# Attention and feed-forward on one core: attention first and alone, x kept in DRAM, feed-forward after it

## The chip, the cores and the metric

The kernel runs on one core of a Trainium2 chip. The core has five engines with a queue of their own each: PE (matrix multiply, with its weight loads shown as PEld), DVE (vector), ACT (scalar functions), POOL, and SP, which here only issues DMAs. They are kept in step by semaphores. Matmuls write to PSUM, eight banks of 512 fp32 values for each of 128 partitions; everything else lies in SBUF. The metric is the device time of one execution in microseconds (us); lower is better.

## The reference

```python
def phi(x):                                    # q, k: 8 x 8 heads x 576 x 64; w_phi: 64 x 128
    proj = np.einsum('bhsd,df->bhsf', x, w_phi)
    proj = proj - np.max(np.abs(proj), axis=-1, keepdims=True)
    return np.concatenate([np.exp(proj), np.exp(-proj)], axis=-1)
q_p, k_p = (phi(q), phi(k))
kv = np.einsum('bhsf,bhsd->bhfd', k_p, v)
z = np.sum(k_p, axis=2)
num = np.einsum('bhsf,bhfd->bhsd', q_p, kv)
den = np.einsum('bhsf,bhf->bhs', q_p, z)[..., None] + 1e-06
x = num / den                                  # as 4608 tokens x 512
h = x @ w_in                                   # 512 x 2048
g = h * np.tanh(np.log1p(np.exp(h)))           # Mish
out = g @ w_out                                # 2048 x 512
```

The weights of the feed-forward come as float64.

## The kernel before

**Attention** is cut into 36 units of 512 (token, head pair) rows of k and 36 of q; two units of q make one chunk c of 256 tokens. A unit of k is loaded and projected into PSUM (`pp_k`, `project`, L158), DVE takes the row maximum of the absolute value (`m`, L173) and subtracts it (`e`, L174), ACT makes both exponentials (L215, L216), and PE sums exp times v into `kvps` (`k_sum`, L183; v has a column of ones, which gives z). A finished pair's `kvps` is copied to `kv` (L232). A unit of q is projected the same way (`pp_q`), turned by PE (`dt`, `q_turn`, L250), put through both exponentials (L252), multiplied with `kv` into `num` (`q_num`, L183), divided (`r`, L267 and L268; `x`, L269), and turned once more into `xt` (`q_out`, L277). ACT and DVE split `xt` into a rounded part `xTh` and a rest `xTl`, which stay in SBUF.

**The feed-forward** works on 18 chunks times 16 tiles f of 128 hidden columns, 288 tiles in all. `ff_in` (L299) makes a tile of `h` with 12 matmuls of 256 columns: four pieces of x, times three products of high and low parts. For each pair of tiles `mish` (L302) has ACT compute Mish into `u` and round it to `gh`, and DVE take the rest `gl` (L312). `ff_out` (L329), LAG tiles later, adds g times w_out into two banks `o`: 6 matmuls of 512 columns a tile.

**The weights** are 32 pieces of 128 x 512 float64 numbers. `split_weight` (L109) makes a high and a low fp32r part of one piece: ACT takes the absolute value of the upper words (L118), DVE clamps, shifts, masks and joins (L120 to L126), ACT rounds (L130), DVE subtracts and adds (L134, L135). For the first 16 pieces (`summed`) the last two are done by PE instead (`sum_weight`, L139: matmuls with the identity into a bank, copied out by ACT).

**Order.** Only PE's order is written out by hand: every piece of work gets a time in tiles (`at`), the events are sorted, and PE runs them in that order. The other engines' orders come out of a scheduler at build time. FIRST_STEPS, WLOADS and WTIMES place the first attention steps and the weights; from the fourth unit on, one unit of attention goes with 8 tiles of the feed-forward, so the two are interleaved to the end. The first two chunks go through the feed-forward in halves of 8 tiles (NHALVED), with partial sums in `part`, as the later weights come late.

**PSUM** has three pools: four banks `ps_att`, two `ps_h` (one pair of h tiles in each bank), two `ps_o`.

Of the kernel before, what the change touches and what calls it, by code (L numbers as in the profile page):

```python
# [52 lines left out]
def attention_then_mish(ctx, tc, qT, kT, va, w_phi, w_in, w_out, out):  # L53
# [15 lines left out]
    nc.sync.dma_start(w_phi2, w_phi)


    pieces = [("in", i, 0) for i in range(NCC)]
    for j in range(1, 4):
        pieces += [("out", 4 * (j - 1) + i, 0) for i in range(4)] + [("in", i, j) for i in range(NCC)]
    pieces += [("out", 12 + i, 0) for i in range(4)]
    weight = {}
    starting = True

    spare = [f"w{kind}_{i}_{j}" for kind, i, j in pieces[-NSPARE:]]

    def slot_tile(slot, dtype, name):
        return const.tile([P, 2, 512], dtype, tag=slot, name=name)

    def spare_tile(n, dtype, name):
        return slot_tile(spare[n], dtype, name)

    ident_r = spare_tile(0, F32R, "ident_r")[:, :, :P]
    for k in range(2):
        nc.scalar.activation(ident_r[:, k, :], ident, AF.Copy, scale=1.0 - 2 * k)
    raws = {}  # L90

    def raw_tile(name):

        n = len(raws)
        raws[n] = None
        if n >= NRAWSPARE:
            return work.tile([P, 512], F32, tag="raw", name=name, bufs=NRAW)
        if n % 2 == 0:
            raws[n] = spare_tile(1 + n // 2, F32, name)
        return (raws[n] if n % 2 == 0 else raws[n - 1])[:, n % 2, :]  # L100

    def load_weight(kind, i, j):
        nm = f"{kind}_{i}_{j}"
        src = w_in[i * P:(i + 1) * P, j * 512:(j + 1) * 512] if kind == "in" else w_out[i * P:(i + 1) * P, :]
        words = slot_tile(f"w{nm}", U32, f"words_{nm}").rearrange("p a b -> p (a b)")
        nc.sync.dma_start(words, src.bitcast(U32))
        weight[kind, i, j] = words.rearrange("p (a b) -> p a b", b=2)

    def split_weight(kind, i, j, summed):  # L109


        nm = f"{kind}_{i}_{j}"
        words = weight[kind, i, j]
        low, high = words[:, :, 0], words[:, :, 1]
        w = moe.tile([P, 512], U32, tag="u", name=f"w_{nm}", bufs=3)
        t = work.tile([P, 512], F32, tag="half", name=f"t_{nm}", bufs=NHALF)
        wf = w.bitcast(F32)
        nc.scalar.activation(wf, high.bitcast(F32), AF.Abs)  # L118

        nc.vector.tensor_scalar(wf, wf, LARGE, SMALL, op0=ALU.min, op1=ALU.max)  # L120
        nc.vector.tensor_scalar(w, w, 3, 0x3FFFFFF8, op0=ALU.logical_shift_left, op1=ALU.bitwise_and)
        nc.vector.scalar_tensor_tensor(w, high, 0xC0000000, w, op0=ALU.bitwise_and, op1=ALU.bitwise_or)

        nc.vector.tensor_scalar(t.bitcast(U32), w, 0xFF800000, None, op0=ALU.bitwise_and)
        rest = work.tile([P, 512], F32R, tag="part", name=f"rest_{nm}", bufs=2 * NHALVED) if summed else t
        nc.vector.scalar_tensor_tensor(rest, low, 2.0 ** -52, t, op0=ALU.mult, op1=ALU.mult)  # L126
        parts = slot_tile(f"w{nm}", F32R, f"w{nm}")
        hi, lo = parts[:, 0, :], parts[:, 1, :]
        weight[kind, i, j] = (hi, lo)
        nc.scalar.copy(hi, wf)  # L130
        if summed:
            to_sum[kind, i, j] = (wf, rest)
        else:
            nc.vector.tensor_sub(wf, wf, hi.bitcast(F32))  # L134
            nc.vector.tensor_tensor(lo, wf, rest, op=ALU.add)  # L135

    to_sum = {}

    def sum_weight(kind, i, j):  # L139
# [3 lines left out]
        nc.tensor.matmul(ps, ident, wf, start=True, stop=False)
# [14 lines left out]
    def project(raw, name, nh):  # L158


        ps = []
        for j in range(2):
            pool, tag = (ps_h, "h") if starting and not nh or j < nh else (ps_att, "att")
            ps.append(pool.tile([P, 4, F], F32, tag=tag, name=f"pp{j}_{name}"))
        for n in range(4):
            for j in range(2):
                rows = slice(j * D, (j + 1) * D)
                nc.tensor.matmul(ps[j][:, n], raw[rows, n * P:(n + 1) * P], w_phi2[rows], start=True, stop=True)  # L168
# [10 lines left out]
    def halves(ps, lhsT, rhs, start, stop):  # L179

        for h in range(2):
            rows = slice(h * D, (h + 1) * D)
            nc.tensor.matmul(ps[rows], lhsT[:, rows], rhs[h], start=start, stop=stop, skip_group_check=True)  # L183
# [245 lines left out]
```

## Time and profile before

| | us |
|---|---|
| median of 3 runs | 1193.73 |
| lowest and highest run | 1188.72, 1194.0 |
| span of the profiled execution | 1190.0 |
| PE busy, PEld busy | 1142.8, 1022.0 |
| ACT busy, DVE busy | 621.4, 480.7 |

Of the profiled execution itself the span is what the profile gives, from its first instruction to its last; it lies among the runs. The profile lists busy time of each engine, the same for any stretch of the span, groups of instructions by source line (`L299 PE MATMUL h<-xTh,win`: line, engine, operation, what is written and read), waits (who waited, and what released him), and the chain that ended last, followed back from the last instruction. In the timeline a row is: start, duration, engine, line, operation, tiles, shapes, count, and in brackets the idle time before it with its releaser. "x16" counts instructions as the chip runs them: an fp32 matmul counts two. Neighbouring operations of an engine overlap, so the distance from start to start is often shorter than the duration.

### The profile page before, as it was taken

What the parts mean: (1) busy time and instruction counts of PE and PEld (TensorE: products, weight loads), DVE (VectorE), ACT (ScalarE), POOL (GpSimd) and SP (SyncE); (2) the same over time, 40 slices, a digit from 0 to 9 for tenths busy, and PEclk for the clock granted to TensorE, in tenths of its full rate; (3) what the DMA queues carried; (4) which work ended last, traced back from release to release, by engine and by line L of the source; (5) the groups of instructions that cost most, each with busy time, mean ns of one, the idle gap of its engine ahead of it and who ended that gap; (6) DMA issues with size and microseconds to landing.
All of it is one profiled execution on the core that took longest, in us unless ns stands there. A gap on an engine that the chain in (4) does not pass through costs nothing.

```text
span 1190.0 us, 26544 instructions
## 1 busy us (share of the span) xinstructions
PE 1142.8 (96%) x11696; PEld 1022.0 (86%) x11696; DVE 480.7 (40%) x1057; ACT 621.4 (52%) x1019; POOL 0.7 (0%) x6
## 2 busy tenths in 40 slices
PE   6888887999999999999999999999999999999998
PEld 5666777999898989898989899989989898898997
DVE  5876987333333333333333333333333332222311
ACT  4567675454555555555555555554545454545422
POOL 0000000000000000000000000000000000000000
PEclk9999987999999999999999999999999999999999
DMA  9901200111111010111111111011111100000000
GB/s 346 375 13 30 74 14 19 48 48 31 48 30 48 27 42 19 41 31 48 30 38 30 48 30 48 19 45 34 34 44 30 48 19 28 1 19 19 1 19 18
DMA packets 25027, 57.51 MB, mean 48 GB/s; under 512 B 2768, under 2 KB 2896, under 8 KB 24912
## 3 DMA queue, kind: packets, MB, share of 16 engines
q1 hardware_dynamic: 24912, 55.81, 14.2%
q8 instruction: 92, 1.51, 0.5%
q14 instruction: 23, 0.19, 0.1%
HBM read 46.37 MB, written 9.44 MB: 47 GB/s over the span
## 4 chain that ended last, share of the span: by engine, by line
PE 83%; ACT 9%; DVE 6%; issue 1%; DMA 1%; SPq 0%; ACTq 0%
PE h L299 32%; PE o L329 29%; PE kvps L183 6%; PE num L183 5%; PE pp_q L168 3%; PE pp_k L168 3%; PE dt L250 2%; ACT L252 2%; ACT e_q L252 1%; PE xt L277 1%; ACT e_k L215 1%; ACT gh L311 1%; ACT u L307 1%; ACT e_k L216 1%; ACT L307 1%
## 5 line engine op out<-in xcount | busy, mean ns | idle before, releaser
L299 PE MATMUL h<-xTh,win 128*128 128x256 f32 x2304 | 465.1, 286 | 8.5 <-DVE e_q L174 5.3
L299 PEld LDWEIGHTS h<-xTh,win 128*128 128x128 f32 x2304 | 377.0, 191 | 22.6 <-issue 5.9
L329 PE MATMUL o<-wout,gh 128*128 128x512 f32 x1152 | 371.8, 404 | 5.5 <-ACT osb L342 4.0
L312 DVE TENSOR_TENSOR gl<-u,gh 128x256 fp32r<-128x256 f32 x288 | 116.7, 424 | 573.0 <-ACT gh L311 564.7
L299 PE MATMUL h<-xTl,win 128*128 128x256 f32 x1152 | 325.9, 283 | 0.0
L329 PEld LDWEIGHTS o<-wout,gh 128*128 128x128 f32 x1152 | 198.7, 190 | 39.1 <-ACT osb L342 9.3
L329 PE MATMUL o<-wout,gl 128*128 128x512 f32 x576 | 228.3, 396 | 0.0
L299 PEld LDWEIGHTS h<-xTl,win 128*128 128x128 f32 x1152 | 219.5, 191 | 8.3
L307 ACT ACTIVATE u<-h 128x512 f32<-128x512 f32 x144 | 86.2, 599 | 171.2 <-PE h L299 165.8
L280 ACT CAST xTh<-xt 128x512 fp32r<-128x512 f32 x36 | 21.2, 589 | 292.3 <-PE xt L277 283.8
L329 PEld LDWEIGHTS o<-wout,gl 128*128 128x128 f32 x576 | 108.9, 189 | 27.4
L311 ACT CAST gh<-u 128x256 fp32r<-128x256 f32 x288 | 110.5, 408 | 19.3 <-PE o L329 6.4
L307 ACT ACT_TABLE_LOAD x73 | 93.7, 1283 | 8.3 <-DVE wout L135 7.0
L183 PEld LDWEIGHTS kvps<-v,e_k 128*64 128x64 f32 x2560 | 82.5, 144 | 13.4 <-issue 11.6
L183 PE MATMUL kvps<-v,e_k 128*64 128x65 f32 x2560 | 87.6, 230 | 0.9 <-ACT e_k L216 0.9
L252 ACT ACTIVATE e_q<-dt 128x512 f32<-128x512 f32 x144 | 77.9, 597 | 16.7 <-PE dt L250 16.4
L252 ACT ACT_TABLE_LOAD x64 | 82.1, 1283 | 1.0
L183 PE MATMUL num<-kv,e_q 128*64 128x65 f32 x2304 | 74.1, 222 | 0.0
L183 PEld LDWEIGHTS num<-kv,e_q 128*64 128x64 f32 x2304 | 70.6, 138 | 2.7 <-issue 2.0
L168 PE MATMUL pp_k<-w_phi,kraw 64*128 64x128 f32 x576 | 49.2, 295 | 20.6 <-issue 9.4
L168 PEld LDWEIGHTS pp_k<-w_phi,kraw 64*128 64x128 f32 x576 | 43.9, 202 | 23.7 <-issue 19.4
L173 DVE TENSOR_REDUCE m_q<-pp_q 128x4 f32<-128x512 f32 x72 | 46.4, 685 | 8.2 <-PE pp_q L168 8.2
(66 smaller groups left out, 756.8 us busy)
## 6 DMA issues: line engine op xcount, KB each, us to landing
v<-va SPq DMA_DIRECT2D x32, 325.0 KB, 3.1
kraw<-kT SPq DMA_DIRECT2D x36, 256.0 KB, 2.7
out<-osb SPq DMA_DIRECT2D x36, 256.0 KB, 2.0
qraw<-qT SPq DMA_DIRECT2D x35, 256.0 KB, 3.0
words_in<-w_in SPq DMA_DIRECT2D x16, 512.0 KB, 8.7
words_out<-w_out SPq DMA_DIRECT2D x16, 512.0 KB, 9.1
kraw<-qT SPq DMA_DIRECT2D x1, 256.0 KB, 8.5
w_phi<-w_phi SPq DMA_DIRECT2D x1, 64.0 KB, 1.7
```

The lines of the kernel that those rows point to most:

```text
L168: nc.tensor.matmul(ps[j][:, n], raw[rows, n * P:(n + 1) * P], w_phi2[rows], start=True, stop=True)
L173: nc.vector.tensor_reduce(m, ps[j], axis=AX.X, op=ALU.max, apply_absolute_value=True)
L183: nc.tensor.matmul(ps[rows], lhsT[:, rows], rhs[h], start=start, stop=stop, skip_group_check=True)
L215: table(nc.scalar.activation(e[:, 1, :], e[:, 0, :], AF.Exp))
L250: nc.tensor.transpose(ps[:, n * P:(n + 1) * P], e[:, 0, n * P:(n + 1) * P], ident)
L252: table(nc.scalar.activation(e[:, s, :], ps, AF.Exp, scale=2.0 * s - 1.0))
L280: nc.scalar.copy(hi, ps)
L299: nc.tensor.matmul(ps, w[:, wcol], x[:, cc % 2, :], start=(n == 0), stop=(n == 11))
L307: table(nc.scalar.activation(u, hv, AF.Mish))
L311: nc.scalar.copy(gh, u[:, f * CH:(f + 1) * CH])
L312: nc.vector.tensor_sub(gl, u[:, f * CH:(f + 1) * CH], gh.bitcast(F32))
L329: nc.tensor.matmul(ps, g[:, cols], w, start=(i == first and k == 0), stop=(i == end and k == 2))
```

## The change

Attention is now run by itself, in 36 steps of 7.3 us (STEP) in PE's hand-written order, with k three units (LEAD) ahead of q. x is turned, copied to SBUF by ACT and stored in a DRAM tile per chunk; the feed-forward loads it back 12 tiles ahead and splits it 6 tiles ahead. The feed-forward follows as one sequence of 288 tiles. Sixteen weight pieces (w_in of j = 0 and 1, w_out of f = 0 to 7) are loaded and split during attention, the other sixteen after it, into a pool that takes over attention's SBUF. All 32 are summed on DVE; `sum_weight` is gone. Four chunks (NSPLIT) go in halves.

A projection now takes a tile of two banks for both heads (`ps_a`, two tiles), and max, subtraction and exponentials run over 1024 elements at once. The `h` of four tiles f share such a two-bank tile. The other four banks (`ps_b`) hold kvps, dt, num and xt, and later o. `gh` and `gl` are made for a pair of tiles at once. The copy to `kv` goes to ACT.

```diff
-NRAW, NE, NV, NKV = 4, 6, 2, 10
-NHALF, NX, NXT, NG = 2, 2, 4, 4
...
-LAG, TAIL, TAILLAG = 4, 10, 2
+LEAD = 3
+STEP = 7.3
+TILE = 2.82
+LAG = 5
+NSPLIT = 4
...
-    ps_att = ctx.enter_context(tc.tile_pool(name="ps_att", bufs=4, space=PSUM))
-    ps_h = ctx.enter_context(tc.tile_pool(name="ps_h", bufs=2, space=PSUM))
-    ps_o = ctx.enter_context(tc.tile_pool(name="ps_o", bufs=2, space=PSUM))
+    ps_a = ctx.enter_context(tc.tile_pool(name="ps_a", bufs=2, space=PSUM))
+    ps_b = ctx.enter_context(tc.tile_pool(name="ps_b", bufs=4, space=PSUM))
...
+    x_spill = [tc.dram_tile([P, NCC, CH], F32, name=f"x_spill_{c}") for c in range(NCH)]
...
-    def sum_weight(kind, i, j):
...
-    def project(raw, name, nh):
+    def project(raw, name):
+
+        ps = ps_a.tile([P, 2, 4, F], F32, tag="pp", name=f"pp_{name}")
         for n in range(4):
             for j in range(2):
                 rows = slice(j * D, (j + 1) * D)
-                nc.tensor.matmul(ps[j][:, n], raw[rows, n * P:(n + 1) * P], w_phi2[rows], start=True, stop=True)
...
+                nc.tensor.matmul(ps[:, j, n], raw[rows, n * P:(n + 1) * P], w_phi2[rows], start=True, stop=True)
+        e = att.tile([P, 2, 2, 512], F32, tag="e", name=f"e_{name}", bufs=5)
+        m = att.tile([P, 2, 4], F32, tag="m", name=f"m_{name}", bufs=4)
+        nc.vector.tensor_reduce(m, ps, axis=AX.X, op=ALU.max, apply_absolute_value=True)
+        nc.vector.tensor_tensor(e[:, :, 0, :].rearrange("p j (n f) -> p j n f", f=F), ps,
+                                m.unsqueeze(3).broadcast_to([P, 2, 4, F]), op=ALU.subtract)
...
-                    nc.vector.tensor_copy(kv[p // NHP, p % NHP], kv_ps.pop(p))
+                    nc.scalar.copy(kv[p // NHP, p % NHP], kv_ps.pop(p))
...
-        nc.scalar.copy(hi, ps)
-        nc.vector.tensor_sub(lo, ps, hi.bitcast(F32))
-        xT[c, g] = (hi, lo)
+        xs = att.tile([P, 2, CH], F32, tag="xs", name=f"xs_{n}", bufs=3)
+        nc.scalar.copy(xs, ps)
+        nc.sync.dma_start(x_spill[c][:, 2 * g:2 * g + 2, :], xs)
...
+    def x_load(c):
+        x32 = ffn.tile([P, NCC, CH], F32, tag="x32", name=f"x32_{c}", bufs=2)
+        nc.sync.dma_start(x32, x_spill[c])
+        xT[c] = x32
+
+    def x_split(c, again):
+        x32 = xT[c]
+        hi = ffn.tile([P, NCC, CH], F32R, tag="xTh", name=f"xTh_{c}_{again}", bufs=2)
+        lo = ffn.tile([P, NCC, CH], F32R, tag="xTl", name=f"xTl_{c}_{again}", bufs=2)
+        nc.scalar.copy(hi, x32)
+        nc.vector.tensor_sub(lo, x32, hi.bitcast(F32))
+        xT[c] = (hi, lo)
...
+    for u in range(NU):
+        t = (u - LEAD) * STEP
+        at(t - 2 * STEP, k_load, u)
+        at(t - STEP, v_load, u)
+        at(t, k_proj, u)
+        at(t + 0.1, k_exp, u)
+        at(t + STEP + 2.0, k_sum, u)
+        t = u * STEP
+        at(t - 2 * STEP, q_load, u)
+        at(t + 1.0, q_proj, u)
+        at(t + STEP + 6.3, q_turn, u, 0)
+        at(t + STEP + 6.8, q_turn, u, 1)
+        at(t + 2 * STEP + 4.0, q_num, u)
+        at(t + 3 * STEP + 6.0, q_out, u)
+    early = [("in", i, j) for j in range(2) for i in range(NCC)]
+    early = [p for n in range(8) for p in (early[n], ("out", n, 0))]
+    for n, pc in enumerate(early):
+        at((2 * n - 2) * STEP + 3.0, load_weight, const, *pc)
+        at((2 * n + 1) * STEP + 3.0, split_weight, const, *pc)
...
+    start = NU * STEP
+    closing = start + 3.5 * STEP
+
+    def close():
+        nonlocal late
+        att_scope.close()
+        late = ctx.enter_context(tc.tile_pool(name="late", bufs=1, reuse_waits="tile"))
+
+    at(closing, close)
+    later = [("in", i, j) for j in range(2, 4) for i in range(NCC)]
+    later = [p for n in range(8) for p in (later[n], ("out", 8 + n, 0))]
+    for n, pc in enumerate(later):
+        at(closing + 0.1 + n * 0.5, lambda *pc: load_weight(late, *pc), *pc)
+        at(closing + 4 + n * 4.0, lambda *pc: split_weight(late, *pc), *pc)
...
+            at(t - 12 * TILE, x_load, c)
+            at(t - 6 * TILE, x_split, c, half)
+        at(t, ff_in, c, f)
         if f % 2:
-            at(n + 0.01, mish, c, f // 2)
-        at(n + 0.5 + LAG + min(max(0, n - total + TAIL), TAILLAG), ff_out, c, f)
+            at(t + 0.1, mish, c, f // 2)
+        at(t + (0.5 + LAG) * TILE, ff_out, c, f)
```

How the engines' rows stand now. In a row are the line, the operation, the tile written, the tiles read (with buffer numbers) and the shape.

**DVE, one step of attention.** Before, around the first unit of chunk 4 and the k unit beside it, in the new kernel for k 13 and q 10 of the projections and q 8 of num. Before:

```order
L269 TENSOR_TENSOR x_0_3498<-num_4_0_3499,r_4_0_3516 128x256
L267 TENSOR_SCALAR r_4_0_3537<-num_4_0_3520 128x4
L268 RECIPROCAL r_4_0_3537<-r_4_0_3537 128x4
L269 TENSOR_TENSOR x_0_3498<-num_4_0_3520,r_4_0_3537 128x256
L173 TENSOR_REDUCE m_q_1_3552<-pp_q_1_3541 128x4
L173 TENSOR_REDUCE m_q_1_3556<-pp_q_1_3542 128x4
L174 TENSOR_TENSOR e_q_1_3551<-pp_q_1_3541,m_q_1_3552 128x512
L174 TENSOR_TENSOR e_q_1_3555<-pp_q_1_3542,m_q_1_3556 128x512
L173 TENSOR_REDUCE m_k_3570<-pp_k_3559 128x4
L173 TENSOR_REDUCE m_k_3574<-pp_k_3560 128x4
L174 TENSOR_TENSOR e_k_3569<-pp_k_3559,m_k_3570 128x512
L174 TENSOR_TENSOR e_k_3573<-pp_k_3560,m_k_3574 128x512
```

And in the changed kernel:

```order
L112 TENSOR_REDUCE m_k_1570<-pp_k_1560 128x8
L113 TENSOR_TENSOR e_k_1569<-pp_k_1560,m_k_1570 128x2x512
L112 TENSOR_REDUCE m_q_1589<-pp_q_1579 128x8
L113 TENSOR_TENSOR e_q_1588<-pp_q_1579,m_q_1589 128x2x512
L198 TENSOR_SCALAR r_8_1655<-num_8_1638 128x4
L199 RECIPROCAL r_8_1655<-r_8_1655 128x4
L200 TENSOR_TENSOR x_1637<-num_8_1638,r_8_1655 128x256
L198 TENSOR_SCALAR r_8_1676<-num_8_1659 128x4
L199 RECIPROCAL r_8_1676<-r_8_1676 128x4
L200 TENSOR_TENSOR x_1637<-num_8_1659,r_8_1676 128x256
```

The division now comes last in a step, behind both projections, and each subtraction stands directly behind the maximum that it needs.

**PE, the same step.** In the changed kernel the rows from one xt to the next num are these (before, 8 tiles of h and o stand between them):

```order
L209 MATMUL xt_1536<-ident,x_1493 128x128 x4
L180 MATMUL dt_8_1544<-ident,e_q_1298 128x128 x4
L180 MATMUL dt_8_1551<-ident,e_q_1298 128x128 x4
L109 MATMUL pp_k_1560<-w_phi_71,kraw_1283 128x128 x8
L109 MATMUL pp_q_1579<-w_phi_71,qraw_1412 128x128 x8
L121 MATMUL kvps_1456<-v_1139,e_k_1423 64x65 x16
L121 MATMUL kvps_1610<-v_1285,e_k_1423 64x65 x24
L121 MATMUL num_8_1638<-kv_605,e_q_1298 64x65 x8
```

Both dts stand ahead of the next step's projections, and nothing of the feed-forward stands between the steps.

**DVE, the early weights.** Rows 86 to 94 of the changed kernel's 774 on DVE:

```order
L112 TENSOR_REDUCE m_k_433<-pp_k_423 128x8
L93 TENSOR_SCALAR t_in_1_3217<-w_in_1_3216 128x512
L99 TENSOR_TENSOR w_out_0_2926<-w_out_0_2926,parts_out_0_2934 128x512
L112 TENSOR_REDUCE m_q_450<-pp_q_440 128x8
L89 TENSOR_SCALAR w_out_0_3504<-w_out_0_3504 128x512
L113 TENSOR_TENSOR e_k_432<-pp_k_423,m_k_433 128x2x512
L94 SCALAR_TENSOR_TENSOR t_in_1_3217<-words_in_1_2782,t_in_1_3217 128x512
L100 TENSOR_TENSOR parts_out_0_2934<-w_out_0_2926,t_out_0_2927 128x512
L113 TENSOR_TENSOR e_q_449<-pp_q_440,m_q_450 128x2x512
```

The sixteen early splits stand closely around the first eight units of k and five of q; the last row of the last one is row 149. Before, the last split's end is row 320 of 1059, among work of the feed-forward.

**ACT, the first late splits.** Rows 260 to 269 of the changed kernel on ACT, at the first of the sixteen later pieces (`L251` is Mish, `L254` the rounding to gh, `L87` the absolute value of the split, `L98` its rounding):

```order
L251 ACTIVATE u_0_5443<-h_0_5412 128x512
L254 CAST gh_0_5445<-u_0_5443 128x512
L87 ACT_TABLE_LOAD
L87 ACTIVATE w_in_2_5491<-words_in_2_5453 128x512
L98 CAST parts_in_2_5499<-w_in_2_5491 128x512
L251 ACT_TABLE_LOAD
L251 ACTIVATE u_1_5527<-h_0_5412 128x512
L87 ACT_TABLE_LOAD
L87 ACTIVATE w_out_0_5543<-words_out_0_5455 128x512
L254 CAST gh_1_5529<-u_1_5527 128x512
```

Each absolute value now stands between two Mishes with a table load on either side; there are 24 such loads between rows 262 and 346. In the whole kernel there are 28, before 145.

More of the change, by code (lines that the diff above doesn't have):

```diff
@@ L69, in attention_then_mish @@
[L69 to L135, printed above, removed]
@@ L194, in k_load @@
     def k_load(n):
-        k_live[n] = raw_tile(f"kraw_{n}")
+        k_live[n] = att.tile([P, 512], F32, tag="kraw", name=f"kraw_{n}", bufs=3)
         nc.sync.dma_start(k_live[n], kT[n])
@@ L251, in q_turn, with q_proj, q_num @@
+    def q_proj(n):
+        q_live[n] = project(q_live.pop(n), f"q_{n}")
+    def q_turn(n, j):
+        e = q_live[n][:, j]
+        ps = ps_b.tile([P, 512], F32, tag="b", name=f"dt{j}_{n}")
+        for i in range(4):
+            nc.tensor.transpose(ps[:, i * P:(i + 1) * P], e[:, 0, i * P:(i + 1) * P], ident)
         for s in range(2):
             table(nc.scalar.activation(e[:, s, :], ps, AF.Exp, scale=2.0 * s - 1.0))
-    def q_num(c, g):
-        es = q_live.pop((c, g))
-        x = x_live[c, g] = work.tile([P, 2, 2, P], F32, tag="x", name=f"x_{c}_{g}", bufs=NX)
+    def q_num(n):
+        c, g = divmod(n, 2)
+        es = q_live.pop(n)
+        x = x_live[n] = att.tile([P, 2, 2, P], F32, tag="x", name=f"x_{n}", bufs=3)
@@ L257, in q_num @@
         for i in range(2):
-            ps = ps_att.tile([P, 2, 2, VW], F32, tag="att", name=f"num{i}_{c}_{g}")
+            ps = ps_b.tile([P, 2, 2, VW], F32, tag="b", name=f"num{i}_{n}")
             for t in range(2):
@@ L332, in ff_out @@
             if f < NFT - 1:
-                part_live[c, tt] = work.tile([P, DM], F32, tag="part", name=f"part_{c}_{tt}", bufs=2 * NHALVED)
+                part_live[c, tt] = late.tile([P, DM], F32, tag="part", name=f"part_{c}_{tt}", bufs=2 * NSPLIT)
                 nc.scalar.copy(part_live[c, tt], ps)
                 continue
-            o = work.tile([P, DM], F32, tag="half", name=f"osb_{c}_{tt}", bufs=NHALF)
+            o = ffn.tile([P, DM], F32, tag="osb", name=f"osb_{c}_{tt}", bufs=3)
             if parts == 2:
                 nc.vector.tensor_tensor(o, ps, part_live.pop((c, tt)), op=ALU.add)
-            elif c == NCH - 1 and tt:
+            elif tt:
                 nc.vector.tensor_copy(o, ps)
@@ new lines, in attention_then_mish @@
+    early = [("in", i, j) for j in range(2) for i in range(NCC)]
[3 more added lines that the diff above has]
+        at((2 * n + 1) * STEP + 3.0, split_weight, const, *pc)
+    tiles = [(c, half * NFT // 2 + f) for half in range(2) for c in range(NSPLIT) for f in range(NFT // 2)]
+    tiles += [(c, f) for c in range(NSPLIT, NCH) for f in range(NFT)]
+    start = NU * STEP
@@ L391, in attention_then_mish @@
+    seen = set()
+    for n, (c, f) in enumerate(tiles):
+        t = start + n * TILE
+        half = f // (NFT // 2) if c < NSPLIT else 0
+        if (c, half) not in seen:
+            seen.add((c, half))
+            at(t - 12 * TILE, x_load, c)
+            at(t - 6 * TILE, x_split, c, half)
+        at(t, ff_in, c, f)
         if f % 2:
-            at(n + 0.01, mish, c, f // 2)
-        at(n + 0.5 + LAG + min(max(0, n - total + TAIL), TAILLAG), ff_out, c, f)
+            at(t + 0.1, mish, c, f // 2)
+        at(t + (0.5 + LAG) * TILE, ff_out, c, f)
```

197 lines of the change are left out of this document (70 added, 127 removed).

## The prediction

> **What bounds the kernel now.** I read the engines' sums first, then busy time by stretch, then the chain that ended last.
>
> ```profile
> PE 1142.8 (96%) x11696; PEld 1022.0 (86%) x11696; DVE 480.7 (40%) x1057; ACT 621.4 (52%) x1019; POOL 0.7 (0%) x6
> ...
> 0.00:5.00 5.00, 0.87 (x8) 0.90 (x10) 0.00 (x0) 1.79 (x3) 0.70 (x6) 1.00 0.56 178
> 5.00:10.00 5.00, 1.21 (x12) 0.91 (x10) 0.69 (x1) 0.52 (x1) 0.00 (x0) 1.00 0.88 275
> 10.00:20.00 10.00, 6.70 (x82) 5.94 (x82) 9.83 (x20) 5.78 (x11) 0.00 (x0) 1.00 1.03 409
> ...
> 140.00:160.00 20.00, 14.72 (x193) 12.85 (x188) 18.80 (x39) 9.60 (x15) 0.00 (x0) 0.83 0.15 45
> ...
> 180.00:200.00 20.00, 14.63 (x188) 12.89 (x187) 16.69 (x39) 11.91 (x19) 0.00 (x0) 0.76 0.05 15
> ...
> 300.00:400.00 100.00, 99.33 (x1018) 89.73 (x1017) 33.01 (x74) 53.05 (x87) 0.00 (x0) 1.00 0.12 38
> ```
>
> In a row of stretches PE comes first, then weight loads, DVE, ACT, POOL, the granted clock, the DMA share and GB/s. From 200 us on PE is full at clock 1.00; before that it is held back where DVE is nearly full (18.80 of 20) with the weight splits, and the clock dips. So the floor is PE's work, and the question is how much of it the first stage leaves idle.
>
> ```profile
> 1141.24 2.85 PE h L299 x24
> 1144.09 2.79 PE o L329 x12
> ...
> 1176.42 9.82 PE o L329 x42
> 1186.27 0.69 DVE osb L340
> ```
>
> In the chain (start, us, what) two feed-forward tiles cost 2.85 + 2.79, or 2.82 a tile; over the 35.18 us from 1141.24 to 1176.42 I count 168 h and 66 o matmuls, which gives 2.81. The 288 tiles are **809 us** in both kernels. After PE's last matmul (1186.24) come 3.8 us to the span's end at 1190.0.
>
> **The change part by part.** *Removed:* the sums of split weights on PE.
>
> ```profile
> 92.80 1.02 PE L143 MATMUL lo_out<-w_out,ident 128*128 128x512 f32 x2
> ...
> 94.12 0.64 PE L329 MATMUL o<-wout,gh 128*128 128x512 f32 x2
> ```
>
> One sum took PE from 92.80 to 94.12: 16 x 1.32 = 21 us less PE work, while DVE gets two operations (0.60 each, below) for each of the 16. The switches of ACT's tables between exp and Mish mostly go too; ACT, at 52%, was no bound. The copy of each finished kv moves from DVE to ACT, which then has two exps of k, four of q and two copies in a step, some 5 us of 8.
>
> *Attention alone: PE.* One step (a unit of k and one of q) costs PE, from start to start:
>
> ```profile
> 224.80 2.55 PE L183 MATMUL kvps<-v,e_k 128*64 128x65 f32 x80
> 227.18 2.04 PE L183 MATMUL num<-kv,e_q 128*64 128x65 f32 x64
> 229.15 1.16 PE L168 MATMUL pp_q<-w_phi,qraw 64*128 64x128 f32 x16
> 230.14 1.23 PE L168 MATMUL pp_k<-w_phi,kraw 64*128 64x128 f32 x16
> 231.30 0.38 PE L299 MATMUL h<-xTh,win 128*128 128x256 f32 x1
> ...
> 1106.27 0.44 PE xt L277 x4
> ...
> 1110.96 0.44 PE dt L250 x4
> ```
>
> kvps 2.38 for 80, so 2.1 for the mean of 71; num 1.97; two projections 2.1; dt 0.9; xt 0.4: 7.5 us.
>
> *Attention alone: DVE.* DVE overlaps neighbours, so cadences count, not durations.
>
> ```profile
> 133.28 1.28 DVE L173 TENSOR_REDUCE m_k<-pp_k 128x4 f32<-128x512 f32 x2
> 134.47 0.68 DVE L122 SCALAR_TENSOR_TENSOR w_in<-words_in,w_in 128x512 uint32<-128x512 uint32 x1
> ...
> 144.62 0.42 DVE L121 TENSOR_SCALAR w_out<-w_out 128x512 uint32<-128x512 uint32 x1
> 144.96 0.42 DVE L120 TENSOR_SCALAR w_out<-w_out 128x512 f32<-128x512 f32 x1
> ...
> 27.26 0.43 DVE L120 TENSOR_SCALAR w_in<-w_in 128x512 f32<-128x512 f32 x1 [3.18 <-ACT w_in L118]
> 27.72 0.43 DVE L121 TENSOR_SCALAR w_in<-w_in 128x512 uint32<-128x512 uint32 x1
> ...
> 228.33 0.16 DVE L267 TENSOR_SCALAR r<-num 128x4 f32<-128x4 f32 x1 [2.37 <-PE num L183]
> 228.53 0.18 DVE L268 RECIPROCAL r<-r 128x4 f32<-128x4 f32 x1
> 228.74 0.42 DVE L269 TENSOR_TENSOR x<-num,r 128x256 f32<-128x256 f32 x1
> ...
> 230.34 1.29 DVE L173 TENSOR_REDUCE m_q<-pp_q 128x4 f32<-128x512 f32 x2 [0.24 <-PE pp_q L168]
> ```
>
> Two reduces of 512 elements take 1.19 (0.60 each), short operations 0.34; one that needs its neighbour's result starts 0.46 after it, 0.12 later. From 0.16 for 4 elements to 0.68 for 512 the slope is 1.02 ns, so a two-bank operation of 1024, which this trace does not show, is estimated at 0.60 + 0.52 = 1.12 (at most two of the old, 1.20). In the new order DVE runs m_k, e_k, m_q, e_q (each e waits for its m: 2 x (1.24 + 1.12) = 4.72), then twice r, reciprocal, x: 0.20 + 0.21 + 0.34 + 0.20 + 0.21 + 0.42 = 1.58.
>
> Here PE's order closes a **loop**. The last dt of a step takes the bank that the second x has just left (four banks hold kvps, two nums, xt and two dts), and the next pp_k stands behind that dt. pp_k start to m_k start 1.19 (229.15 to 230.34), DVE 4.72 + 1.58, then dt 0.44 and about 0.07 of semaphores: **8.0 us a step**, over PE's 7.5. Bounds: 7.5 (another bank is free) to 8.4 (old widths, more latency).
>
> *The first 100 us.* The order shows all 16 early splits within DVE's first 149 operations, not over 32 steps. The first weight is now ninth in SP's queue.
>
> ```profile
> 9.48 0.66 ACT L118 ACTIVATE w_in<-words_in 128x512 f32<-128x512 f32 x1 [6.94 <-DMA words_in<-w_in]
> ```
>
> Up to it 2.64 MB are loaded; at 178, 275 and 409 GB/s that is 10.9 us, after the 0.66 of ACT 11.8 (9.48 + 0.69 before). From there to the x of the third unit DVE has 48 x 0.34 + 64 x 0.60 = 54.7 of splits, 11 m and 12 e at 1.12 (25.8) and six r-reciprocal-x groups (4.5): 85. With 3 for waits (0 if ACT keeps up, 20 if PE, idle and at half clock, comes late) pp_k of step 5 starts at **100 us**. That is where the old kernel, too, loses time; the change moves the loss, since DVE does more here (no PE sums).
>
> *From there:* 28 steps with both k and q x 8.0 = 224, two x splits on DVE inside the loop 2.2; three steps without k, in which num waits for the four exps of dt just issued, 6.5 + 5.6 + 5.6 = 18. In the last two, PE has pp_q 1.07, waits 1.0, num 2.0, then 1.1 for DVE's r and x with an e_q among them, and dt 0.44. Feed-forward begins at 344.
>
> *Feed-forward:* 809, plus the attention work left among its first tiles (2 num, 3 xt, 2 dt: 6.2) and 1.3 of waiting for exps. The spare o banks (four for two) take the old wait for an o bank away.
>
> *DRAM.* 36 stores of 0.26 MB and 22 loads of 0.52 MB are new, 21 MB over the run or 18 GB/s, against 409 moved at 10 to 20 us.
>
> ```profile
> kraw<-kT SPq DMA_DIRECT2D x36, 256.0 KB, 2.7
> ```
>
> A store waits on SP for ACT's copy, and the k, q and v loads of later steps are queued behind it. They are issued three steps (24 us) before their use and land in 2.7; x is read 12 tiles (34 us) ahead. That cover hides both, and I cost them at nothing; without it each step would wait the 2.7, 28 x 2.7 = 76 us.
>
> *Late splits.* They start at tile 10, as the late pool waits for attention's last use, and the last piece of j = 3 is needed at tile 36: 26 x 2.81 + 1 = 74 us later. DVE has 15 x 3.42 + 11 gl x 0.60 + 4 x 1.12 = 62 us. ACT now changes tables between Abs and Mish 24 times there.
>
> ```profile
> 132.76 1.28 ACT L307 ACT_TABLE_LOAD   x1 [0.17 <-DVE win L135]
> 134.06 0.60 ACT L307 ACTIVATE u<-h 128x512 f32<-128x512 f32 x1
> 134.55 0.58 ACT L334 COPY part<-o 128x512 f32<-128x512 f32 x1
> ```
>
> A load takes 1.30 to the next start (132.76 to 134.06) and an operation of 512 columns 0.49. 24 loads are 31 us, and 62 such operations (abs, casts, Mish, part copies) and four x casts of double width 34: 65 of 74. DVE waits for ACT in the first splits, where each abs stands behind a load; following the two orders against each other I find about 4. So DVE needs 66 and ACT 65 of 74, and I take 2 us of PE waiting, nearer to nothing. Bounds: 0, and 17 (PE lost 5.3 of 20 us at 140 to 160 under a like load, here over 65 us).
>
> **Sum:** 344 + 6.2 + 1.3 + 809 + 2 + 3.8 = 1166 to 1167 against the span of 1190.0. The median of the runs, 1193.7, lies 3.7 above that span, so the forecast is **1171**.
>
> **Rivals.**
> 1. *PE bounds the steps*: another bank is free and the loop does not close; 28 x 0.5 = 14 less, 1157. For it: kvps holds no bank in every ninth step. Against: the new order gives dt a wait on DVE in nearly all steps.
> 2. *The late splits are not hidden*: ACT and DVE at 69 and 66 of 74 us hold gl or the j = 3 weights back; 15 more, 1186. For it: the rows at 140 and 180 us.
> 3. *The clock falls in attention (slower).* The place is the end of each step, 1.3 us of transposes and 0.5 of waiting.
>
> ```profile
> 32.81 1.13 PE L168 MATMUL pp_k<-w_phi,kraw 64*128 64x128 f32 x14 [0.52 <-DVE e_k L174]
> ...
> 35.19 3.81 PE L183 MATMUL kvps<-v,e_k 128*64 128x65 f32 x72 [0.87 <-ACT e_k L216]
> ...
> 50.26 0.63 PE L250 MATMUL dt<-ident,e_q 128*128 128x128 f32 x4 [0.39 <-DVE r L267]
> ...
> 51.63 0.44 PE L277 MATMUL xt<-ident,x 128*128 128x128 f32 x2 [0.15 <-DVE x L269]
> 52.00 2.09 PE L183 MATMUL num<-kv,e_q 128*64 128x65 f32 x64
> ```
>
> After gaps of 0.52 and 0.87 within 3 us the kvps took 53 ns each against 32 at 224.80: half speed. It decides from about 1.4 us of idleness in 3.4: one slow stretch of 3.4 us a step loses 1.7, 28 x 1.7 = 48, so 1219. Against it: the transposes at 50 to 52 us, with gaps of 0.39 and 0.15, left the num behind them at full speed (2.09, as 2.04 later).
> The Trainium skill ("TensorE: Matmul & The Clock Gate", Part 4: PE-mode transpose) says that transposes do not count as busy for the clock gate; by it 1.8 idle us a step would pass the point and 1219 would be the sum. The num at 52.00 speaks against it.
> 4. *A table switch costs twice its load*: if ACT pauses as long again at each of the 24 switches, it needs 96 of 74 us and the first tiles wait for it; about 31 more, 1202 (slower). Against: Mish starts 1.30 after the start of a load of 1.28, and the load began 0.17 after its release, so no pause of that length has room.
> The Trainium skill ("ScalarE: Activation LUTs", What ACT_TABLE_LOAD costs) does put a drain of about 1.38 us on top of each load; the row at 132.76 does not show it.
> 5. *It doesn't do what it says*: half the weights are to be split across attention, but all stand in its first 100 us; if PE at half clock there keeps DVE waiting the full 20, nothing is gained: 1188 to 1190.
>
> **Chances.** Forecast 0.51 (own range 1160 to 1182), rival 1 0.17, rival 2 0.15, rival 3 0.08, rival 4 0.02, rival 5 0.07. A measurement tells about 0.5% from no change (1187.8 to 1199.7). Faster: 0.51 + 0.17 and half of rival 2, 0.75; slower: rivals 3 and 4, 0.10; the same: the other half of rival 2 and rival 5, 0.15. The range 1150 to 1200 goes from rival 1 with a shorter start to rivals 2 and 5 with their bounds, and leaves out rivals 3 and 4.
>
> **What would show it.** Right: from 100 to 330 us steps 8.0 apart with PE's dt waiting for DVE's x and clock 1.0; DVE near full up to 100 us; the first h of tile 0 near 344; PE full from then. Rival 1: steps of 7.5 and no dt wait. Rival 2: idle PE before h or o between 410 and 450 us, released by gl or parts. Rival 3: clock under 0.9 in attention. I am wrong if DVE waits for PE or DMA in the first 100 us, or if 1024-wide operations cost over 1.2.

## The result and the profile after

| | before | changed |
|---|---|---|
| median of 5 runs, us | 1192.76 | 1198.23 |
| lowest and highest run, us | 1188.72, 1194.0 | 1197.32, 1201.74 |
| ratio, 95% interval | 1 | 1.0061 [1.004, 1.0082] |
| span of the profiled execution, us | 1190.0 | 1200.0 |

The change makes the kernel a little slower: forecast was 1171. (The profiled execution of the changed kernel is the longest of its five runs, 1201.74 us, 3.5 above the median, so its parts below add up to a little more than the median does.) The page of the changed kernel begins with the engines' sums, and busy time by stretch (columns as before: PE, weight loads, DVE, ACT, POOL, clock, DMA share, GB/s) shows where PE stands still.

```profile
PE 1122.3 (94%) x11632; PEld 1017.9 (85%) x11632; DVE 471.0 (39%) x772; ACT 458.7 (38%) x708; POOL 0.7 (0%) x6
...
0.00:50.00 50.00, 27.76 (x424) 25.37 (x424) 41.56 (x69) 22.20 (x30) 0.70 (x6) 0.83 0.75 278
50.00:100.00 50.00, 30.70 (x546) 28.07 (x546) 47.01 (x89) 25.77 (x44) 0.00 (x0) 0.76 0.22 64
100.00:150.00 50.00, 43.05 (x926) 39.48 (x926) 33.97 (x54) 26.66 (x41) 0.00 (x0) 0.93 0.44 142
...
200.00:250.00 50.00, 47.25 (x1072) 42.60 (x1070) 36.55 (x60) 29.84 (x47) 0.00 (x0) 1.00 0.42 130
...
390.00:470.00 80.00, 65.60 (x375) 57.59 (x374) 60.11 (x112) 63.12 (x81) 0.00 (x0) 0.91 0.23 87
...
500.00:600.00 100.00, 100.00 (x639) 90.87 (x638) 21.40 (x29) 24.43 (x39) 0.00 (x0) 1.00 0.11 38
```

PE's work fell by 20.5 us, as forecast (1142.8 to 1122.3), yet PE is idle for longer. Three stretches lose: the first 100 us, where DVE is nearly full; attention, where PE has 47 of 50 us in the steady steps; and, unexpected, 390 to 470 us, in the feed-forward, where PE, DVE and ACT all have idle time (14.4, 20 and 17 of 80) and the clock is 0.91. Outside of these PE is nearly full at clock 1.00 (356 to 390 us: 34.0 of 34; 470 to 500: 29.4 of 30).

Two marks divide the span. The timeline of PE gives the start of step 5 and the first h:

```profile
97.97 1.16 PE L109 MATMUL pp_k<-w_phi,kraw 64*128 64x128 f32 x16
...
331.17 1.16 PE L109 MATMUL pp_k<-w_phi,kraw 64*128 64x128 f32 x16
...
356.09 0.36 PE L243 MATMUL h<-xTh,parts_in 128*128 128x256 f32 x1
```

| part of the span | forecast | measured | off by |
|---|---|---|---|
| to step 5 | 100 | 98.0 | -2.0 |
| 28 steps with k (98.0 to 339.6) | 226.2 | 241.6 | +15.4 |
| three steps without k | 18 | 16.5 | -1.5 |
| first h to the end | 822.3 | 843.9 | +21.6 |

(331.17 is the last step with k; at the steady period it ends at 339.57. Of the 822.3 us, 2 were for the late splits, so the stage without any loss is taken as 820.3, and 843.9 is 23.6 above it.) Two terms failed: the steps, and the cover of the late splits. PE's waits, summed over the run, name both (who waited, for whom, us, times, longest); of the 17.9 us before dt, 9.7 lie in the steps from 98 to 339 us:

```profile
PE dt L180 <- DVE r L198: 17.9, 15, 7.7
PE h L243 <- ACT u L251: 15.0, 6, 4.3
```

**A step.** In the chain of work (start, us, what) one whole step reads:

```profile
306.03 1.12 PE pp_k L109 x16
...
307.17 1.24 DVE m_k L112
...
308.50 1.23 DVE e_k L113
309.72 1.14 DVE m_q L112
...
310.96 1.22 DVE e_q L113
312.18 0.08 DVE r L198
...
312.50 0.42 DVE x L200
...
313.06 0.64 PE dt L180 x4
...
313.81 0.63 PE dt L180 x4
314.43 1.12 PE pp_k L109 x16
```

This is the loop of the prediction, 8.40 us long. The four DVE operations take 4.93 (4.72 forecast), from 307.17 to 312.10, where by the timeline r starts while e_q still ends (the chain shows r only from e_q's end). The first dt begins 0.14 after the first x ends (312.92); the profile names r as its releaser, since the second r ends in between. The second x ends at 313.66 by the timeline, the second dt begins 0.15 later, and the next pp_k comes 1.37 after the first dt. Clock is 1.00 from 139 to 339 us, so rival 3 did not happen.

**Two steps are longer**, 11.63 us from 97.97 and 10.89 from 118.21. They hold the x casts of the first two chunks:

```profile
103.67 1.05 ACT L227 CAST xTh<-x 128x1024 fp32r<-128x1024 f32 x1 [4.27 <-DMA x<-x_spill]
104.62 1.05 ACT L147 ACTIVATE e_k<-e_k 128x1024 f32<-128x1024 f32 x1
...
107.08 0.65 PE L209 MATMUL xt<-ident,x 128*128 128x128 f32 x4 [2.70 <-ACT kv L163]
...
123.48 1.05 ACT L227 CAST xTh<-x 128x1024 fp32r<-128x1024 f32 x1 [3.48 <-DMA x<-x_spill]
```

ACT waits 4.27 us in its queue for a load that nobody needs for 250 us; the exponentials of k and the copy of kv stand behind it, and PE behind that copy. The steps behind these two take 8.61 and 9.58 us, and the clock from 98 to 139 us is 0.92; the four together are 7.1 us over four of 8.40.

**The late splits.** ACT's timeline before two of PE's longest waits for u:

```profile
419.90 0.59 ACT L278 COPY part<-o 128x512 f32<-128x512 f32 x1 [3.07 <-PE o L273]
420.51 1.28 ACT L251 ACT_TABLE_LOAD   x1
421.81 0.60 ACT L251 ACTIVATE u<-h 128x512 f32<-128x512 f32 x1
...
424.45 1.28 ACT L87 ACT_TABLE_LOAD   x1
425.75 0.66 ACT L87 ACTIVATE w_out<-words_out 128x512 f32<-128x512 f32 x1
426.42 1.28 ACT L251 ACT_TABLE_LOAD   x1
427.72 0.60 ACT L251 ACTIVATE u<-h 128x512 f32<-128x512 f32 x1
...
457.72 1.28 ACT L251 ACT_TABLE_LOAD   x1 [1.49 <-DVE parts_out L100]
459.01 0.60 ACT L251 ACTIVATE u<-h 128x512 f32<-128x512 f32 x1
```

PE's rows that these release, and what the waiting does to its speed:

```profile
428.37 0.58 PE L243 MATMUL h<-xTh,parts_in 128*128 128x256 f32 x1 [4.32 <-ACT u L251]
...
459.66 0.39 PE L243 MATMUL h<-xTh,parts_in 128*128 128x256 f32 x1 [4.11 <-ACT u L251]
```

From 420.51 to 428.3 ACT is never idle, and three loads are 3.8 of these 7.8 us. Before 457.72 ACT waits for something else: Mish writes `u`, and the split's `w` takes turns in the same three buffers (both have `tag="u"`), so Mish waits until DVE has finished a piece. PE waits, since the bank of four h tiles comes free only when Mish has read both pairs. It never waits for a weight here. The six waits make 15.0 of the 23.6 us. PE also works at clock 0.50 for some 11 us behind the three longest (399.0 to 402.4, 428.4 to 433.1 and 460.5 to 463.8), which costs an estimated 6 more.

### The profile page after: what moved, and what is told of

It reads as the page before. It is cut to its first block, busy times and chain, and to the rows that moved or that the text cites. A ratio compares the mean times of both kernels' runs of the same rounds, so it can differ in the third digit from the quotient of the medians.

```text
span 1200.0 us, 25819 instructions
## 1 busy us (share of the span) xinstructions
PE 1122.3 (94%) x11632; PEld 1017.9 (85%) x11632; DVE 471.0 (39%) x772; ACT 458.7 (38%) x708; POOL 0.7 (0%) x6
## 3 DMA queue, kind: packets, MB, share of 16 engines
q1 hardware_dynamic: 33264, 76.79, 18.7%
## 4 chain that ended last, share of the span: by engine, by line
PE 72%; DVE 19%; ACT 3%; DMA 3%; issue 2%; SPq 1%; DVEq 0%; ACTq 0%
PE h L243 32%; PE o L273 31%; PE dt L180 3%; DVE e_q L113 3%; DVE m_k L112 3%; DVE e_k L113 3%; PE pp_k L109 3%; DVE m_q L112 3%; DMA words_out<-w_out 2%; PE num L121 1%; DVE x L200 1%; ACT L251 1%; PE kvps L121 1%; DMA x<-x_spill 1%; PE pp_q L109 1%
## 5 line engine op out<-in xcount | busy, mean ns | idle before, releaser
L243 PE MATMUL h<-xTh,parts_in 128*128 128x256 f32 x2304 | 459.2, 284 | 15.0 <-ACT u L251 15.0
L243 PEld LDWEIGHTS h<-xTh,parts_in 128*128 128x128 f32 x2304 | 378.2, 192 | 28.7 <-ACT u L251 17.5
L273 PE MATMUL o<-parts_out,gh 128*128 128x512 f32 x1152 | 363.6, 397 | 0.0
L243 PE MATMUL h<-xTl,parts_in 128*128 128x256 f32 x1152 | 326.9, 284 | 0.0
L255 DVE TENSOR_TENSOR gl<-u,gh 128x512 fp32r<-128x512 f32 x144 | 99.5, 691 | 486.5 <-ACT gh L254 486.4
L251 ACT ACTIVATE u<-h 128x512 f32<-128x512 f32 x144 | 86.1, 598 | 517.2 <-PE h L243 517.1
L243 PEld LDWEIGHTS h<-xTl,parts_in 128*128 128x128 f32 x1152 | 221.1, 192 | 10.0
L273 PE MATMUL o<-parts_out,gl 128*128 128x512 f32 x576 | 224.8, 390 | 0.0
L273 PEld LDWEIGHTS o<-parts_out,gh 128*128 128x128 f32 x1152 | 201.2, 191 | 27.7
L273 PEld LDWEIGHTS o<-parts_out,gl 128*128 128x128 f32 x576 | 109.1, 189 | 24.9
L254 ACT CAST gh<-u 128x512 fp32r<-128x512 f32 x144 | 89.4, 621 | 3.8
L180 PE MATMUL dt<-ident,e_q 128*128 128x128 f32 x288 | 45.6, 286 | 29.4 <-DVE r L198 17.9
## 6 DMA issues: line engine op xcount, KB each, us to landing
words_in<-w_in SPq DMA_DIRECT2D x16, 512.0 KB, 10.1
```

Source lines behind the costliest of these rows:

```text
L180: nc.tensor.transpose(ps[:, i * P:(i + 1) * P], e[:, 0, i * P:(i + 1) * P], ident)
L243: nc.tensor.matmul(ps, w[:, wcol], x[:, cc, :], start=(n == 0), stop=(n == 11))
L251: table(nc.scalar.activation(u, hv, AF.Mish))
L254: nc.scalar.copy(gh.rearrange("p f s -> p (f s)"), u)
L255: nc.vector.tensor_sub(gl.rearrange("p f s -> p (f s)"), u, gh.rearrange("p f s -> p (f s)").bitcast(F32))
L273: nc.tensor.matmul(ps, g[:, cols], w, start=(i == first and k == 0), stop=(i == end and k == 2))
```

## The experiments

Twelve kernels were run, each in several rounds beside the kernel before. "To h" is the start of the first h, "from h" the span's rest, both of the profiled execution. The kernel before took 1189.3 to 1192.8 us in the median beside them, so 2 or 3 us between medians of different rounds say nothing.

| run | median, us | ratio to before, 95% | to h | from h |
|---|---|---|---|---|
| changed kernel | 1198.23 | 1.0061 [1.004, 1.0082] | 356.1 | 843.9 |
| e1_late_abs | 1183.96 | 0.9955 [0.994, 0.997] | 354.1 | 828.1 |
| e2_w_own | 1188.41 | 0.9986 [0.9973, 0.9999] | 353.1 | 833.4 |
| e3_turn_late | 1270.43 | 1.0684 [1.0665, 1.0702] | 420.3 | 850.9 |
| e4_x_ordered | 1192.01 | 1.0016 [1.0004, 1.0029] | 347.9 | 842.6 |
| e5_turn_exp | 1176.34 | 0.9879 [0.9864, 0.9894] | 325.9 | 847.9 |
| e6_late_both | 1183.63 | 0.9939 [0.9924, 0.9954] | 352.4 | 828.7 |
| e7_all | 1164.63 | 0.978 [0.9763, 0.9796] | 326.9 | 834.2 |
| e8_spread | 1140.77 | 0.9581 [0.9567, 0.9595] | 304.5 | 834.4 |
| e9_due | 1133.27 | 0.9525 [0.9511, 0.9539] | 304.1 | 828.0 |
| e10_actload | 1125.09 | 0.9457 [0.9442, 0.9473] | 296.8 | 826.6 |
| e11_spread_only | 1206.2 | 1.0132 [1.0113, 1.0151] | 360.0 | 845.1 |
| e12_late_due | 1176.4 | 0.9895 [0.9868, 0.9922] | 350.8 | 822.1 |

### Why Mish is late: loads or buffers

First the loads (e1_late_abs):

```diff
-        nc.scalar.activation(wf, high.bitcast(F32), AF.Abs)
+        if pool is const:
+            nc.scalar.activation(wf, high.bitcast(F32), AF.Abs)
+        else:
+            nc.vector.tensor_scalar(w, high, 0x7FFFFFFF, None, op0=ALU.bitwise_and)
```

Then the buffers (e2_w_own):

```diff
-        w = ffn.tile([P, 512], U32, tag="u", name=f"w_{nm}", bufs=3)
+        w = ffn.tile([P, 512], U32, tag="w", name=f"w_{nm}", bufs=2)
```

> The absolute value of the sixteen late pieces is taken by DVE (a bitwise and, about 0.4 us each) instead of ACT, so that ACT loads no table between two Mishes. In the changed kernel PE stands about 24 us in the feed-forward, nearly all before h, waiting for ACT's u. Theory A (ACT is late because of its 24 table loads, 31 us): the loss falls to 8 us or less, time 1178 to 1184. Theory B (Mish is late because the split's w and Mish's u take turns in the same three buffers, so that Mish waits for DVE's split whatever ACT does): the loss stays at 17 us or more, time 1191 to 1199.

> The split's w gets two buffers of its own, so that Mish's three u buffers are Mish's alone; ACT still loads 24 tables. Theory A (table loads): no change beyond 4 us, 1194 to 1202. Theory B (shared buffers): the loss of 24 us falls by at least 12, time 1174 to 1187.

The stage from h fell to 828.1 without the loads (loss 7.8 of 23.6) and to 833.4 with the buffers parted (loss 13.1). Theory A's first number is met, but its second, no change by the buffers, is not; theory B alone is refuted by e1, and its 12 us for e2 were 10.5. The edit of e1 takes the sixteen absolute values themselves from ACT along with the loads, and the two are not told apart. The gains, 15.8 and 10.5, make more than the loss they come from, which fits that partly they are the same us: either a load or a blocked buffer is enough to hold the next Mish back. PE's wait for u, 15.0 us in the changed kernel, in e1 and then in e2 (380 to 500 us; the line numbers shift by 3 with e1's edit):

```profile
PE h L246 <- ACT u L254: 3.7, 3, 2.3
```

```profile
PE h L243 <- ACT u L251: 5.5, 2, 3.2
```

Both edits together:

> No table loads among the late splits and buffers of their own for w; attention as in the changed kernel. PE's loss in the feed-forward was 24 us, 8 with the loads taken away, 13 with the buffers alone. If the two causes are independent, the loss goes to 3 us or less: 1175 to 1179. If they are one wait seen twice (ACT standing in order behind DVE's split), the loss stays at 6 to 8: 1181 to 1184.

The stage takes 828.7, no less than with e1 alone, as the second theory had it in time. But it is not the same wait that remained; the waits of e6 have no u any more, and this instead:

```profile
PE h L246 <- ACT parts_in L101: 2.2, 1, 2.2
...
PE h L246 <- DVE parts_in L103: 1.5, 1, 1.5
```

With Mish on time, PE reaches the last w_in pieces before DVE has split them. So in e12_late_due, with the edits of e1 and e2, the order of the pieces was changed too:

```diff
-    later = [p for n in range(8) for p in (later[n], ("out", 8 + n, 0))]
+    later = later + [("out", 8 + n, 0) for n in range(8)]
```

> The changed kernel with the late splits alone mended: no table loads, buffers of its own for w, and the late pieces in the order of PE's need; attention as in the changed kernel. In the run of 1183.6, with the first two, PE stood 4 us before h for parts and ran at a clock of 0.89 to 0.94 after it, all between 440 and 480 us. If the order of the pieces is what is left of the loss: no wait of h for parts, 6 to 7 us less, 1176 to 1178, and the stage from the first h on takes 821 to 823 as against 843.9 in the changed kernel. If DVE is short in any order: 1181 to 1184.

Median 1176.4, from h 822.1, and PE is full where it stood (windows of e12):

```profile
400.00:420.00 20.00, 20.00 (x129) 18.18 (x129) 18.67 (x38) 9.18 (x15) 0.00 (x0) 1.00 0.01 4
...
440.00:460.00 20.00, 20.00 (x129) 18.16 (x128) 16.60 (x31) 8.74 (x15) 0.00 (x0) 1.00 0.09 27
```

DVE does the same splits, and one operation more per piece, 18.7 of 20 us busy, and hides them. So 21.8 of the 23.6 us were order, ACT's absolute values with their loads, and a shared buffer, not DVE's throughput. Their shares are not parted further.

### The loop of a step

The dts moved behind the next projections (e3_turn_late):

```diff
-        at(t + STEP + 6.3, q_turn, u, 0)
-        at(t + STEP + 6.8, q_turn, u, 1)
+        at(t + 2 * STEP + 1.2, q_turn, u, 0)
+        at(t + 2 * STEP + 1.7, q_turn, u, 1)
```

> Both dts of a step are put behind the next step's two projections in PE's order, so that pp_k no longer stands behind a dt that waits for DVE's x. Theory loop (the step of 8.4 us is the loop pp_k, four DVE operations, the division, dt): it opens, the step falls to PE's own 7.5 to 7.7, the first h comes 20 to 25 us earlier (331 to 336), time 1173 to 1179. Rival (num then waits for ACT's four exponentials that follow the dts at once, or the banks close another loop): steps of 8.2 or more, time 1193 to 1200.

Neither: steps of 10.1 us and 1270. The rival's place is right, its size is not. ACT in one step, and PE's num behind it:

```profile
303.81 1.06 ACT L147 ACTIVATE e_k<-e_k 128x1024 f32<-128x1024 f32 x1 [3.03 <-DVE e_k L113]
304.89 1.06 ACT L148 ACTIVATE e_k<-e_k 128x1024 f32<-128x1024 f32 x1
305.86 2.04 ACT L182 ACTIVATE e_q<-dt 128x512 f32<-128x512 f32 x4
...
306.98 0.82 PE L121 MATMUL num<-kv,e_q 128*64 128x65 f32 x12 [1.33 <-ACT e_q L182]
```

The chain of ACT's activations (`table` keeps them in program order) has k's exponentials ahead of q's, so num now waits for DVE's e_k, which num does not need. The edit opened one loop and closed a longer one: pp_k, m_k, e_k, two exps of k, exps of q, num, x. Putting k_exp behind the dts takes that away (e5_turn_exp, with e3's and, below, e4's edits):

```diff
-        at(t + 0.1, k_exp, u)
+        at(t + 3.0, k_exp, u)
```

> As the run with the dts behind the projections, but k's two exponentials now follow q's four in ACT's order (in the failed run ACT took k's first, which wait for DVE's e_k, and num waited for q's behind them); the x casts are ordered as in the run of 1192.0. Theory loop: steps of 7.5 to 7.8, PE's own work, so 28 x 0.7 = 20 us less than 1192: 1168 to 1175. Rival (another loop over DVE and ACT closes): steps of 8.1 or more, 1184 or above.

Steps are 7.48 and 7.95 by turns, 7.71 in the mean of 26 (98.76 to 299.20), and the first h comes at 325.9, 22.0 before e4's. PE's dt waits for x no more; neighbouring pp_k:

```profile
207.10 1.16 PE L109 MATMUL pp_k<-w_phi,kraw 64*128 64x128 f32 x16
...
214.58 1.16 PE L109 MATMUL pp_k<-w_phi,kraw 64*128 64x128 f32 x16
```

The median is 1 us above the range, as 5 us come back from h on, where more of attention is left among the first tiles.

### The x casts

e4_x_ordered chains them into ACT's order:

```diff
-        nc.scalar.copy(hi, x32)
+        table(nc.scalar.copy(hi, x32))
```

> ACT's cast of x to xTh is chained behind the exponentials and Mishes that stand ahead of it in the program, so the casts of the first two chunks leave the middle of attention, where ACT waited 4.3 and 3.5 us in them for the x load. Theory spill (two steps of 11.6 and 10.9 us, and the slower clock behind them, come from these waits): 6 to 8 us less up to the first h, time 1190 to 1193. Rival (those steps are long for another reason, the last early splits or the clock): no change, 1197 to 1200. The casts then fall in the last steps of attention, where each could cost 1 us.

First h at 347.9, 8.2 earlier, and 6.2 us less in the median. From 97.9 us on no step with k is over 8.41. Among the waits of the changed kernel stands this one, and in e4 none for x_spill:

```profile
ACT xTh L227 <- DMA x<-x_spill: 7.7, 2, 4.3
```

So no other wait for the way over DRAM shows; what cost was that the scheduler put two users of it early into an in-order queue.

### The early splits

e11_spread_only chains the early absolute values alone:

```diff
-        nc.scalar.activation(wf, high.bitcast(F32), AF.Abs)
+        act = nc.scalar.activation(wf, high.bitcast(F32), AF.Abs)
+        if pool is const:
+            table(act)
```

> The changed kernel with one edit: the early absolute values are chained into ACT's order, so that one piece is split in every second step; dt, k's exponentials, x casts and the late splits as changed. Theory loop (DVE's work stands in the loop pp_k, DVE, dt, so a split's 3.5 us lengthen the step by as much): the start gets 36 us shorter and the 16 splits cost 56, first h at 360 to 378, time 1202 to 1222. Rival (DVE has 2.2 us free in each step of 8.4, the splits fit there): first h near 325, 1165 to 1172.

First h at 360.0, time 1206.2: the loop theory, at its lower end. DVE's spare time in a step cannot be used, as PE's dt waits longer for the division (summed over the run, 17.9 in the changed kernel; from 98 to 339 us alone 28.1 for 9.7):

```profile
PE dt L182 <- DVE r L200: 32.5, 21, 2.2
```

Spread alone loses. With the loop open it is the largest gain of all. e7_all joins the edits of e1, e2, e4 and e5; e8_spread adds to e7 the chaining, in e1's branch for the early pieces:

```diff
-            nc.scalar.activation(wf, high.bitcast(F32), AF.Abs)
+            table(nc.scalar.activation(wf, high.bitcast(F32), AF.Abs))
```

> The two runs of this call in one kernel, with the x casts ordered. If the three repairs are independent: 1198 less 20 (step), 8 (x casts) and 22 (late splits), 1146 to 1152. If attention's gain is given back in the feed-forward, 1160 or more.

> The run with all repairs, and the early absolute values chained into ACT's order, so that one early piece is split in every second step instead of all in the first 100 us. Theory (the first 100 us are lost to DVE; spread, DVE needs 6.5 + 1.7 a step and PE 7.6, so that a step takes 8.2 from the start): first h near 36 x 8.2 + 20 = 315 against 326, time about 10 us under the run with all repairs, 1136 to 1142. Rival (a step with a split takes 9.9 and one without 7.6, as two projection tiles give no slack over a step): first h near 335, time 1155 to 1162.

e7 falls short of its range and comes out as its rival had it: to h 326.9, like e5, but from h 834.2; the w_in pieces were late, as in e6, and 5.5 us more went at the seam, where PE has 55.5 of 60 us busy from 300 to 360 and num waits for q's exponentials between table loads. e8 met its time, but partly by luck: the range was set some 10 us below an e7 of 1146 to 1152, and e8 gained 23.9 on an e7 of 1164.6. The first h came earlier than expected, at 304.5 instead of 315, with steps of 7.9 in the mean and not 8.2.

> The run of 1140.8 with the late pieces split in the order in which PE needs them: first the eight of w_in (tiles 32 and 36), then the eight of w_out (one per tile from 37.5 on). In it PE still stood 4 us before h for the last pieces of w_in, with DVE nearly full. If the order alone is at fault: PE does not wait for parts any more, 6 us less, 1133 to 1136. If DVE's work (some 3.8 us a piece) is too much for the window in any order: 1139 to 1142.

> The same, and the early pieces are loaded from ACT's queue, in ACT's order, one in every second step; SP's queue then holds the attention loads alone. In the run of 1140.8 the early pieces' 8.4 MB went ahead of attention's loads in SP's queue, and PE stood 3.7 us for kraw and 4.7 us for v between 23 and 37 us, after which a stretch ran at a clock of 0.83. If those loads are the cause: 9 to 12 us less than the run sent with it, 1122 to 1127. If issuing on ACT holds up the exponentials by as much, no gain.

Both lie in their ranges, though e10's gain on e9, 8.2, is just under the 9 to 12 expected. e9 is e8 with e12's order of the pieces: from h 828.0 for 834.4. e10, built on e9, issues the early loads from ACT, chained into ACT's order and so spread over the steps as well:

```diff
-        nc.sync.dma_start(words, src.bitcast(U32))
+        if pool is const:
+            table(nc.scalar.dma_start(words, src.bitcast(U32)))
+        else:
+            nc.sync.dma_start(words, src.bitcast(U32))
```

In e8 PE had stood for attention's loads behind the weights, twice:

```profile
27.13 2.08 PE L112 MATMUL pp_k<-w_phi,kraw 64*128 64x128 f32 x16 [3.67 <-DMA kraw<-kT]
...
36.49 2.87 PE L124 MATMUL kvps<-v,e_k 128*64 128x65 f32 x48 [4.72 <-DMA v<-va]
```

In e10 the first h comes 7.3 us before e9's, the clock of 20 to 50 us goes from 0.83 to 1.00, and the page says:

```profile
PE 1100.5 (98%) x11632; PEld 1002.4 (89%) x11632; DVE 470.3 (42%) x788; ACT 416.2 (37%) x670; POOL 0.7 (0%) x6
```

At 1125.09 us, 0.9457 [0.9442, 0.9473] of the kernel before, this version beats both kernels, with the change's structure intact.

## Why the prediction was wrong

The direction was wrong, and its sum was off by 33 us of span (27 in the median); the steps that failed add up to that.

- **"Late splits ... I take 2 us of PE waiting, nearer to nothing": failed, 23.6 measured, and this is the step that cost the direction.** It compared busy sums, ACT 65 and DVE 66 of 74 us, and concluded that they fit. They did (63 and 60 of 80 busy at 390 to 470), but work passes to and fro between two in-order queues, with Mish in the middle of one. The DVE waits for ACT that the orders showed were counted in ("I find about 4"), the other directions were not: ACT's casts waiting for DVE, and Mish for a shared buffer (e2), although `tag="u"` stands in both kernels. Even the price of a table load was right, 1.28 each; what was missing is that PE had no slack behind it (e1). With this step alone mended, and steps of 8.40 as before, the kernel takes 1176.4 (e12), faster than the kernel before.
- **Rival 2, 0.15, named this place** with 15 us against 23.6, but another path: ACT and DVE nearly full, and waits for gl or parts. PE waited for u, with both engines idle for 17 and 20 of 80 us. Parts came second, once u was mended (e6, e12). Alone it would have given 1186; the rest came from the steps.
- **"8.0 us a step": right mechanism, mis-sized, 8.40 measured.** The loop and its closing by dt and x are as predicted, and e5, which opens it, finds PE's own 7.5 (7.48 in every second step). Of the 0.4, DVE's four operations give 0.21 (an e starts 1.33 after its m, 1.24 taken), and the way from the second x to pp_k 0.19: by the timeline the second dt begins 0.15 behind x and pp_k (314.36) 0.55 behind that dt, 0.70 where 0.07 and 0.44 were taken. Twenty-eight steps make 11 of the 15.4 us. It lies at the upper bound, 8.4.
- **"Two x splits on DVE inside the loop 2.2": 6.4 measured** as a remainder (the 15.4 less 11.2 plus 2.2; the 7.1 us of the four steps from 98 us, less 0.7 of one shorter step later). The DRAM round trip was costed at nothing because x is read 12 tiles ahead; for the first two chunks the scheduler read it as soon as it was there, and the cast waited in the middle of attention (e4).
- **The first 100 us: right**, 98.0, and for the reason given: from its first split at 11.3 on DVE is busy for 84 of 87 us (85 of 88 forecast). That this is a loss which a better order gives back was only half seen: e11 shows that it can't be had while the loop is closed, e8 that it can when it is open.
- **Right as well:** 21 us less on PE for the sums, a full PE once the late splits are over (from 500 us on), the width of the two-bank operations (cadence 1.14 against 1.12), rivals 3 and 4 absent. Rival 1 was absent for the reason given against it.
- **Rival 5 did happen in its first half** (all early splits stood in the first 100 us) without its price: PE kept DVE waiting there for 0.9 us only, after the first 6.2 before any work.

For rival 3: the Trainium skill ("TensorE: Matmul & The Clock Gate", Part 4: PE-mode transpose) says that a transpose does not count as PE-busy in the way that other matmuls do. So counted, the 1.37 us of dt and the gap of 0.57 before it would be 1.9 idle us in a step, more than the 1.4 from which rival 3 expected half speed; the granted clock was 1.00 from 150 to 330 us, so the measurement decides against it here.

## What to carry to other kernels

Busy sums under 100% do not show that side work is hidden when it passes to and fro between in-order queues: follow one piece through both orders, and list what stands behind each of its waits and whose buffers it shares. Where a closed loop sets a stage's period, time freed elsewhere buys nothing until the loop is open (spreading the early splits alone cost 8 us, 1206.2 against 1198.2; on top of the open loop it gained 24, 1164.6 to 1140.8). When a wait is moved, look at what every other engine's queue now has ahead of the released work: moving dt alone made the step 10.1 us, with k's exponentials moved as well (and the x casts ordered) 7.7.
